# A fused attention and feed-forward kernel: the instruction order of all five engines written as one string, and 267 additions turned into accumulating transfers

## The chip, the cores and the metric

The kernel runs on one core of a Trainium2 chip. The core has five engines with a queue each: TensorE (PE; its weight loads are shown as PEld), VectorE (DVE), ScalarE (ACT), GpSimd (POOL) and SyncE (SP), which here only issues transfers. Each works through its queue in order and waits at the head for what the instruction needs. TensorE writes to PSUM, eight banks of 128 x 512 f32; the others work on SBUF, and all but GpSimd read PSUM as well. Transfers (DMAs) run on 16 transfer engines. The metric is the device time of one execution in microseconds, a median of several.

## The reference

An input x of 4 batches x 12416 rows x 128 channels goes through attention with 32 inducing points and then through a gated feed-forward layer of width 1536. All is float32.

```python
h = mab(I, x)                     # 32 rows per batch: softmax(I x^T / sqrt(C)) x
x = mab(x, h)                     # each row: softmax(x h^T / sqrt(C)) h
rms = sqrt(mean(x * x, -1) + 1e-6)
xn = x / rms * rms_g
g = xn @ w_gate                   # 128 -> 1536
silu = g * (1 / (1 + exp(-g)))
out = (silu * (xn @ w_val)) @ w_out   # 1536 -> 128
```

Since a row of x after the second attention is a weighting of the 32 rows of h, the kernel multiplies h with the gate and value weights once per batch (the stacks sg and sv), and a row then needs only its 32 weights, scaled by the root mean square.

## The kernel before, in words

Each batch b is cut into 7 sets of rows and these into 25 units: 24 of 512 or 480 rows and one of 256. A unit's weights lie in a tile a of 128 x 512: upper and lower halves of the 32 weights, twice, gathered by SyncE (`gather`, L560 on) from the halves that `seam` (L507 on) makes: turned scores, squares with the Gram matrix, a root on GpSimd, a scaling, and a split into an upper and a lower half.

A unit has 12 blocks j, one for each 128 columns of the 1536, 1200 blocks in all. `ffn` (L663 on) makes of each a slot: a gate matmul (L743, one pass, since a and sg are float32r), silu on ScalarE (L751), a value matmul (L754), and the product of silu and value on VectorE (L760). In 14 blocks that lie among the exponentials of attention, silu is put together from tanh (L747) and one more operation on VectorE (L748), so that ScalarE need not change its table.

The product u has then to be multiplied with 128 rows of w_out and summed over the 12 blocks in acc. A table of letters says in which of three ways:

- a dot, 381 blocks: plain. A float32 matmul, which TensorE runs as two instructions of two passes each (L676, acc<-u,wo).
- s, 619 blocks, "sums": u stays in the PSUM bank of the value. ScalarE takes an upper part from it (L725) and VectorE the remainder (L726), both float32r. GpSimd makes a third factor of the two in a third tile (L735). Three one-pass matmuls follow in `project3`: upper and lower into the bank u3 (L700, L702), the third into acc (L676).
- d, 200 blocks, "differences": u lies in SBUF; the upper part is made by ScalarE (L729), the remainder by GpSimd (L730), a scaling of the upper part by ScalarE (L734), and the third factor by GpSimd (L735).

w_out was split in the same way once (`split_wo`, `split_last`). When a unit's 12 products are done, ScalarE takes u3 (L705), VectorE adds acc (L685) and turns the result (L690), and SyncE stores it in four transfers (L717).

The factors u have 9 tiles. The sets of three tiles (upper, lower, third) number 4, and 2 more are lent from the stacks' buffers while the next batch's stacks are not being made. PSUM has 5 banks in turn for gates, values and attention, 2 for acc and 1 for u3.

While batch b goes through the blocks, the attention of batch b + 1 runs beside it in small steps (`attention`, L309 on): turns of the loaded channels, scores, maxima, exponentials, sums, stacks. A step often issues on several engines at once: `scores1` a matmul and VectorE's eviction, `stack` a matmul, a ScalarE copy and a VectorE subtraction, `turn_h` a matmul and two copies. The order is written out: `schedule` and `seams` say which steps there are, `places` in which slot each comes, `ordered` after which part of a slot how many plain and three-pass products are issued, `banks`, `workers` and `holders` which buffer each gets. `soon` and `wait` put a factor's making and a unit's finish one or two slots later.

The opening (`first`, L802 on) does batch 0's attention and rounds the weights, before the first block; the first 24 blocks go through two units side by side.

Of the kernel before, what the change touches and what calls it, by code (L numbers as in the profile page):

```python
# [23 lines left out]
def kernel(  # L24
# [75 lines left out]
    RING, RESERVE, HELD, SILU = 4, 7, 9, 3  # L100
    LENT = (RING, RING + 1)
# [41 lines left out]
    def load_channels(b, s, k):  # L143

        w = R * per[s]
        if not k:
            xT[b, s] = xtp.tile([P, w * m], F32, name=f"xT{s}")
        nc.sync.dma_start(out=xT[b, s][ts(k, m), :].rearrange("p (w c) -> p w c", c=m),
                          in_=xrows[ds(b * N + start[s], P * per[s]), ts(k, m)].rearrange("(i w) c -> i w c", i=m))
# [159 lines left out]
    def attention(b, load_next):  # L309
# [34 lines left out]
        def scores1(s):  # L344
            nc.vector.tensor_scalar(out=sc[b][:, cols1[s]], in0=scores(s, indT[:], R, per[s]), scalar1=1.0, scalar2=None,
                                    op0=ALU.mult, op1=ALU.max, accum_out=st["gmx"][:, s:s + 1])
# [31 lines left out]
        def sum_h(*sets):  # L378
# [12 lines left out]
            if b and sets[0]:  # L391
                nc.vector.tensor_tensor(out=hl[:, 0:C], in0=hl[:, 0:C], in1=ps[:, 0:C], op=ALU.add)
            elif b:
                nc.scalar.copy(out=hl[:, 0:C], in_=ps[:, 0:C])

        def fold_l():

            nc.vector.reduce_sum(out=st["hl"][:, C:C + 1], in_=st["ls"][:, 0:st["n"]], axis=AX.X)
            ps = bank()
            nc.tensor.matmul(ps[:, 0:1], fold[:].rearrange("p q m -> p (q m)"), st["hl"][:, C:C + 1], start=True, stop=True)  # L400
            rl = st["rl"] = small.tile([P, 1], F32, name="rl")
            nc.vector.reciprocal(out=rl[:], in_=ps[:, 0:1])
# [8 lines left out]
        def turn_h():  # L411

            ps = bank()
            nc.tensor.matmul(ps[:, 0:P], st["hn"], fold[:].rearrange("p q m -> p (q m)"), start=True, stop=True)
            hT = st["hT"] = once.tile([P, P], F32, name="hT")
            if b:
                nc.scalar.copy(out=hT[:], in_=ps[:, 0:P])
                hg = st["hg"] = once.tile([P, P], F32, name="hg")
                nc.scalar.activation(hg[:], ps[:, 0:P], AF.Copy, scale=gam)
            else:  # L420
                nc.vector.tensor_copy(out=hT[:], in_=ps[:, 0:P])
# [5 lines left out]
        def square_h():  # L427
# [4 lines left out]
            ps = bank()  # L432
            nc.tensor.matmul(ps[:, 0:m], st["hT"][:], st["hT"][:, 0:m], start=True, stop=True)
            for q in range(R):
                to, of_ = gram[b][ts(q, m), ts(q, m)], ps[ts(q, m), 0:m]
                nc.scalar.activation(to, of_, AF.Copy, bias=1e-6, scale=1.0 / C)

        def scores2(s):
            ps = scores(s, st["hT"][:, 0:m], quarters[s], per2[s])
            nc.vector.transpose(out=sc[b][rows2[s], cols2[s]], in_=ps)  # L440

        def row_max(s):
            mx = st["mx2"] = small.tile([P, 16], F32, name="mx2")[rows2[s], 0:per2[s]]
            nc.vector.reduce_max(out=mx, in_=weights(b, s), axis=AX.X)

        def sub_max(s):
            n, v, mx = per2[s], weights(b, s), st["mx2"]
# [16 lines left out]
        def stack(i):  # L464


            ps = bank()
            for c, w in enumerate(st.pop(("w", i))):
                nc.tensor.matmul(ps[ts(c, m), :], st["hg"][:, 0:m], w, start=True, stop=True)
            hi, lo = st["halves", i] = [worker([P, 512], F32R, n) for n in ("whi", "wlo")]  # L470
            rows = slice(0, NC * m)
            nc.scalar.copy(out=hi[rows, :], in_=ps[rows, :])
            nc.vector.tensor_tensor(out=lo[rows, :], in0=ps[rows, :], in1=hi[rows, :].bitcast(F32), op=ALU.subtract)
# [33 lines left out]
    def seam(b, s):  # L507
# [41 lines left out]
        def split():  # L549
# [4 lines left out]
            else:  # L554
                nc.vector.tensor_copy(out=hi[rows, 0:w], in_=aT[rows, 0:w])
            engine.tensor_tensor(out=lo[rows, 0:w], in0=aT[rows, 0:w], in1=hi[rows, 0:w].bitcast(F32), op=ALU.subtract)

        return [turn_a, square, times, scale, root, apply, turn_b, split]
# [11 lines left out]
    plain, kara, waiting = [], [], []  # L570

    def soon(k, step):

        waiting.append([k, step])

    def wait():

        for one in waiting:
            one[0] -= 1
        while any(not one[0] for one in waiting):  # L580
            one = next(one for one in waiting if not one[0])
            waiting.remove(one)
            one[1]()

    def give(group):

        for kind in group:
            (plain if kind == "p" else kara).pop(0)()

    def split_wo(step):  # L590

        if not step:
            kws["first"] = xnp.tile([P, half + NK, C], F32R, name=f"xn{full - 1}")
            rings = [xnp.tile([P, RING, 512], F32R, name=f"xn{full - 4 + n}") for n in range(3)]
            kws["sets"] = [[ring[:, n, :] for ring in rings] for n in range(RING)]
            idle.extend(range(RING))
# [10 lines left out]
        for g in range(2):  # L607
# [8 lines left out]
            if at == 4:  # L616
                nc.gpsimd.tensor_tensor(out=part(2, g)[0], in0=part(1, g)[1], in1=part(0, g)[1], op=ALU.subtract)
            if at == 6:
                scaled(0, g, 4096.0)

    idle, leaving = [], []

    def lend(b, k, idle, leaving):

        if k == (20 if not b else 2):
            idle += LENT
            return True
        if b + 1 < B and k == 184:
            leaving += [n for n in LENT if n not in idle]
            idle[:] = [n for n in idle if n not in LENT]  # L630
        assert k != 192 or not leaving

    def give_back(n, idle, leaving):

        leaving.remove(n) if n in leaving else idle.append(n)

    def lend_tiles():

        tiles = [stk.tile([P, F], F32R, name=name) for name in ("sg", "sv")]
        kws["sets"][RING:] = [[t[:, ts(n, 512)] for n in range(3)] for t in tiles]  # L640

    def split_last(step):

        n = NJ - NK
        if not step:
            kws["last"] = xtp.tile([P, 3 * n, C], F32R, name="xT0")
        one, (whi, wlo, ws) = wo[:, NK:NJ, :], (kws["last"][:, ts(kind, n), :] for kind in range(3))
        if step == 0:
            nc.scalar.activation(whi, one, AF.Copy, scale=1.0 - 2.0 ** -13)
            nc.gpsimd.tensor_tensor(out=wlo, in0=one, in1=whi.bitcast(F32), op=ALU.subtract)  # L650
        if step == 1:
            nc.scalar.activation(wlo, wlo.bitcast(F32), AF.Copy, scale=4096.0)
            nc.gpsimd.tensor_tensor(out=ws, in0=wlo.bitcast(F32), in1=whi.bitcast(F32), op=ALU.subtract)
        if step == 2:
            nc.scalar.activation(whi, whi.bitcast(F32), AF.Copy, scale=4096.0)

    def weight_of(kind, j):
        if j >= NK:
            return kws["last"][:, kind * (NJ - NK) + j - NK, :]
# [3 lines left out]
    def ffn(b, u):  # L663

        s, q = units[u]
        T = per2[s] * m
        a = moving.pop((b, u))
        sg, sv = stacks[b]
        acc = ps_acc.tile([P, 512], F32, name="acc")
        nk = sum((b, u, j) in kinds for j in range(NJ))  # L670
        st = {"left": NJ, "k": nk}
        if nk:
            st["o"] = None

        def project(lhsT, rhs, to):
            nc.tensor.matmul(to, lhsT, rhs, start=st["left"] == NJ, stop=st["left"] == 1)  # L676
            st["left"] -= 1
# [638 lines left out]
```

## Time and profile before

| | |
|---|---|
| median of 3 runs | 1538.12 us (1537.94 to 1538.22) |
| the profiled execution's own time | 1538.19 us |
| its span, first to last instruction | 1536.4 us |
| granted TensorE clock | 1.00 |
| instructions: VectorE, ScalarE, GpSimd | 2519, 2501, 1158 |
| transfers | 112.58 MB, 36.2% of 16 engines' span, all but a few issued by SyncE |
| the first gate of the feed-forward | 47.5 us after the start |
| the 27th gate | 84.3 us |
| start of batch 1, 2, 3 (its first gate) | 434, 805, 1180 us |

A line of a group reads: line of the kernel, engine, operation, what it writes <- what it reads, shapes, count | busy time, mean of one | idle time of the engine before them, and what ended it. A line of the waits reads: who <- whom: total us, times, the longest. A stage's limit is read from its own stretch, not from the total. A matmul's duration overlaps with the next one; the distance between starts is its price. "gv" are the five PSUM banks, "xn", "sg" and "sv" also name the sets of factors, which lie in buffers that had those names.

### The profile page before, as it was taken

Reading aid. Unit: us, or ns where it says so; the run is one execution under the profiler, and the core shown is the slowest. Engines: PE = TensorE matmul, PEld = TensorE weight load, DVE = VectorE, ACT = ScalarE, POOL = GpSimd, SP = SyncE. Lnnn points to the kernel's source line nnn. Section 1 sums busy time; section 2 is a strip of 40 time slices with the busy share of each in tenths; the row PEclk is TensorE's granted clock in tenths of the full one; section 3 lists DMA queues with packets and bytes.
Section 4 is the critical chain, followed back from the end, with each engine's and each line's share of the span. In section 5 each row is a group of like instructions: output and inputs, shape, how many; then the busy total and the mean of one; then the engine's idle time right before and its main releaser. Section 6 shows DMA issues by size and latency. Waiting matters only on the chain.

```text
span 1536.4 us, 26105 instructions
## 1 busy us (share of the span) xinstructions
PE 1518.3 (99%) x7141; PEld 1091.8 (71%) x7141; DVE 1442.3 (94%) x2519; ACT 1292.2 (84%) x2501; POOL 1418.5 (92%) x1158
## 2 busy tenths in 40 slices
PE   8999999999999999999999999999999999999998
PEld 6556667767776667776777667676677777777776
DVE  6999999999999998999999999899999999999997
ACT  5777889888888889887988888978798888888886
POOL 1379999999999999999999999899989999999997
PEclk9999999999999999999999999999999999999999
DMA  7345535435453242634444323353222222122221
GB/s 282 91 81 94 97 60 114 90 78 91 67 92 69 38 93 37 137 84 86 72 78 82 56 59 77 74 120 75 49 39 39 38 36 37 34 40 38 40 40 28
DMA packets 389331, 112.58 MB, mean 73 GB/s; under 512 B 365088, under 2 KB 369728, under 8 KB 386624
## 3 DMA queue, kind: packets, MB, share of 16 engines
q1 hardware_dynamic: 388592, 110.83, 36.2%
q8 instruction: 57, 0.93, 0.3%
q14 instruction: 90, 0.74, 0.2%
q10 hardware_dynamic: 592, 0.08, 0.0%
HBM read 53.95 MB, written 27.00 MB: 53 GB/s over the span
## 4 chain that ended last, share of the span: by engine, by line
PE 90%; DVE 3%; POOL 3%; ACT 2%; issue 1%; DMA 0%; DVEq 0%; POOLq 0%; ACTq 0%
PE acc L676 30%; PE gv L743 17%; PE gv L754 16%; PE u L700 10%; PE u L702 10%; PE gv L341 3%; PE gv L523 1%; PE gv L390 1%; POOL xn L735 1%; ACT silu L751 1%; PE gv L820 1%; DVE u L760 1%; POOL xn L730 0%; DVE gv L760 0%; DMA xn<-in_x_dram 0%
## 5 line engine op out<-in xcount | busy, mean ns | idle before, releaser
L735 POOL TENSOR_TENSOR xn<-xn,xn 128x512 fp32r<-128x512 f32 (+2 forms) x626 | 767.6, 1248 | 34.1 <-DVE xn L726 11.6
L751 ACT ACTIVATE silu<-gv 128x512 f32<-128x512 f32 (+2 forms) x1186 | 683.4, 588 | 98.4 <-PE gv L743 88.1
L754 PE MATMUL gv<-a,sv 128*128 128x512 f32 (+2 forms) x1188 | 551.2, 465 | 1.0 <-ACT silu L751 0.4
L743 PE MATMUL gv<-a,sg 128*128 128x512 f32 (+2 forms) x1188 | 472.2, 398 | 1.6 <-ACT silu L751 0.6
L760 DVE TENSOR_TENSOR gv<-silu,gv 128x512 f32<-128x512 f32 (+2 forms) x616 | 410.6, 673 | 23.4 <-PE gv L754 7.5
L760 DVE TENSOR_TENSOR u<-silu,gv 128x512 f32<-128x512 f32 (+2 forms) x570 | 369.4, 655 | 24.4 <-ACT silu L751 8.8
L676 PE MATMUL acc<-u,wo 128*128 128x512 f32 (+2 forms) x762 | 371.2, 577 | 0.0
L725 ACT ACTIVATE xn<-gv 128x512 fp32r<-128x512 f32 (+2 forms) x472 | 278.1, 589 | 62.3 <-DVE gv L760 47.2
L726 DVE SCALAR_TENSOR_TENSOR xn<-xn,gv 128x512 fp32r<-128x512 f32 (+2 forms) x472 | 312.5, 662 | 13.1 <-ACT xn L725 7.4
L743 PEld LDWEIGHTS gv<-a,sg 128*128 128x128 f32 x1188 | 224.1, 189 | 137.4 <-issue 26.7
L754 PEld LDWEIGHTS gv<-a,sv 128*128 128x128 f32 x1188 | 224.3, 189 | 116.5 <-ACT silu L751 34.4
L700 PE MATMUL u<-xn,xn 128*128 128x512 f32 (+2 forms) x599 | 233.7, 390 | 0.0
L676 PE MATMUL acc<-xn,more 128*128 128x512 f32 (+2 forms) x599 | 225.7, 377 | 1.4 <-POOL xn L735 1.2
L730 POOL TENSOR_TENSOR xn<-u,xn 128x512 fp32r<-128x512 f32 (+2 forms) x154 | 191.0, 1240 | 5.1 <-ACT xn L729 4.7
L676 PEld LDWEIGHTS acc<-u,wo 128*128 128x128 f32 x762 | 142.9, 190 | 32.2 <-issue 15.4
L700 PEld LDWEIGHTS u<-xn,xn 128*128 128x128 f32 x599 | 113.3, 189 | 25.6 <-ACT o L705 8.0
L676 PEld LDWEIGHTS acc<-xn,more 128*128 128x128 f32 x599 | 113.1, 189 | 24.4 <-POOL xn L735 10.2
L735 POOL TENSOR_TENSOR sg<-sg 128x512 fp32r<-128x512 f32 (+2 forms) x97 | 123.4, 1272 | 3.6 <-DVE sg L726 1.0
L735 POOL TENSOR_TENSOR sv<-sv 128x512 fp32r<-128x512 f32 (+1 forms) x96 | 122.1, 1272 | 1.6 <-DVE xT L324 0.2
L702 PE MATMUL u<-xn,more 128*128 128x512 f32 (+2 forms) x304 | 113.0, 372 | 0.0
L702 PE MATMUL u<-xn,xn 128*128 128x512 f32 (+2 forms) x295 | 109.8, 372 | 0.0
L729 ACT ACTIVATE xn<-u 128x512 fp32r<-128x512 f32 (+2 forms) x154 | 95.3, 619 | 14.2 <-DVE u L760 9.2
(229 smaller groups left out, 1894.7 us busy)
## 6 DMA issues: line engine op xcount, KB each, us to landing
out_dram<-o SPq DMA_DIRECT2D x320, 64.0 KB, 2.0
xT<-in_x_dram SPq DMA_DIRECT2D x60, 256.0 KB, 3.9
xn<-in_x_dram SPq DMA_DIRECT2D x60, 256.0 KB, 5.0
a<-hi SPq DMA_DIRECT2D x156, 64.0 KB, 2.0
a<-lo SPq DMA_DIRECT2D x156, 64.0 KB, 2.0
xn<-in_x_dram SPq DMA_DIRECT2D x5, 1024.0 KB, 9.7
xn<-w SPq DMA_DIRECT2D x18, 256.0 KB, 3.0
out_dram<-o SPq DMA_DIRECT2D x64, 60.0 KB, 2.0
```

What stands on the lines that cost most here:

```text
L676: nc.tensor.matmul(to, lhsT, rhs, start=st["left"] == NJ, stop=st["left"] == 1)
L700: nc.tensor.matmul(ups[:, 0:T], weight_of(0, j), halves_in_turn(hi), start=st["k"] == nk, stop=False)
L702: nc.tensor.matmul(ups[:, 0:T], weight_of(1, j), halves_in_turn(lo), start=False, stop=not st["k"])
L725: nc.scalar.activation(hi, v, AF.Copy, scale=(1.0 - 2.0 ** -13) * 2.0 ** -12)
L726: nc.vector.scalar_tensor_tensor(out=lo, in0=hi.bitcast(F32), scalar=-4096.0, in1=v, op0=ALU.mult, op1=ALU.add)
L729: nc.scalar.activation(d, v, AF.Copy, scale=1.0 - 2.0 ** -13)
L730: nc.gpsimd.tensor_tensor(out=lo, in0=v, in1=d.bitcast(F32), op=ALU.subtract)
L735: nc.gpsimd.tensor_tensor(out=d, in0=hi.bitcast(F32), in1=lo.bitcast(F32), op=ALU.subtract)
L743: nc.tensor.matmul(g[:, 0:T], sg[:, ts(j, P)], halves_in_turn(a[:, 0:T]), start=True, stop=True)
L751: nc.scalar.activation(sl[:, 0:T], g[:, 0:T], AF.Silu)
L754: nc.tensor.matmul(v[:, 0:T], sv[:, ts(j, P)], halves_in_turn(a[:, 0:T]), start=True, stop=True)
L760: nc.vector.tensor_tensor(out=t[:, 0:T], in0=sl[:, 0:T], in1=v[:, 0:T], op=ALU.mult)
```

## The change

1. **Order.** Slots, `soon`, `wait`, `schedule`'s slots and the table of products are gone, but for the first 26 blocks, which keep their order. After these a string `program` of 10,695 letters is run from left to right, and each letter issues one step on one engine: g gate, s silu, y tanh, x the operation after tanh, v value, m product, h upper part, l lower part on VectorE, n lower part on GpSimd, e scaling of the upper part, q two of the three passes, d the third factor by GpSimd, D the third factor by a transfer, r and R the third pass behind d and D, p a plain product, E, F, T, O a unit's four finishing steps, a gather, and a dot for the next of attention's steps by the list `taken`.
2. **Steps of one engine.** Attention's steps that used several engines are split: `scores1` and `evict1`, `scores2` and `turn2`, `sum_h` and `take_h`, `fold_l` in three, `turn_h` and two copies, `square_h` and `copy_gram`, `stack`, `stack_high` and `stack_lower`, and the split of a seam into `split` and `lower`.
3. **Kinds.** `sorts` has a letter for each block: 366 plain, 586 sums (412 S, 174 s), 248 differences (155 D, 93 d). A small letter means that the third factor is made by a transfer: 267 blocks. 28 blocks use tanh.
4. **Third factor in place.** The signs of the upper parts are turned, so that the third factor is the sum of upper and lower part and can be put over the lower part, after the first two passes have read it: by GpSimd (567 blocks), or by a transfer that GpSimd issues and that adds the upper part's 128 x 512 f32 to the lower part in SBUF. A three-pass block thus has two tiles instead of three.
5. **Buffers.** 9 tiles for u and 10 more, 19 in one pool for plain factors, upper and lower parts. Nothing is lent from the stacks. The last split of w_out lies beside them and is made in the opening.

VectorE's lower part is taken from PSUM alone, as before.

```diff
-        RING, RESERVE, HELD, SILU = 4, 7, 9, 3
-    LENT = (RING, RING + 1)
+    RING, HELD, SILU = 4, 9, 3
...
-            rings = [xnp.tile([P, RING, 512], F32R, name=f"xn{full - 4 + n}") for n in range(3)]
-            kws["sets"] = [[ring[:, n, :] for ring in rings] for n in range(RING)]
+            rings = [xnp.tile([P, RING * 512], F32R, name=f"xn{full - 4 + n}") for n in range(3)]
+            kws["room"] = [ring[:, ts(n, 512)] for ring in rings for n in range(RING)][:3 * RING - 2]
...
-                nc.gpsimd.tensor_tensor(out=d, in0=hi.bitcast(F32), in1=lo.bitcast(F32), op=ALU.subtract)
-                kara.append(lambda: project3(j, where))
...
+    def high():
+        n = lists["h"].pop(0)
+        one, kind, t = unit_of(*blocks[n][:2]), kinds[n], factor_of[n]
+        T = one["T"]
+        hi = t["hi"] = room()[:, 0:T]
+        t["lo"] = room()[:, 0:T]
+        if kind in "Dd":
+            nc.scalar.activation(hi, t["u"], AF.Copy, scale=1.0 - 2.0 ** -13)
+            lists["n"].append(n)
+        else:
+            nc.scalar.activation(hi, t["u"], AF.Copy, scale=-(1.0 - 2.0 ** -13) * 2.0 ** -12)
+            lists["l"].append(n)
...
+    def low():
+        nc.vector.scalar_tensor_tensor(out=t["lo"], in0=t["hi"].bitcast(F32), scalar=4096.0, in1=t["u"],
+                                       op0=ALU.mult, op1=ALU.add)
...
+    def low_of_u():
+        nc.gpsimd.tensor_tensor(out=t["lo"], in0=t["u"], in1=t["hi"].bitcast(F32), op=ALU.subtract)
...
+    def project_two():
+        nc.tensor.matmul(ups, weight_of(0, j), halves_in_turn(t["hi"]), start=not one["q"], stop=False)
+        nc.tensor.matmul(ups, weight_of(1, j), halves_in_turn(t["lo"]), start=False, stop=last)
+        one["q"] += 1
+        lists["D" if kinds[n].islower() else "d"].append(n)
...
+    def add_in_place():
+        n = lists["d"].pop(0)
+        t = factor_of[n]
+        nc.gpsimd.tensor_tensor(out=t["lo"], in0=t["hi"].bitcast(F32), in1=t["lo"].bitcast(F32), op=ALU.add)
+        lists["r"].append(n)
+
+    def add_by_transfer():
+        n = lists["D"].pop(0)
+        t = factor_of[n]
+        nc.gpsimd.dma_start(out=t["lo"].bitcast(F32), in_=t["hi"].bitcast(F32), accum_op=ALU.add)
+        lists["R"].append(n)
+
+    def project_third(name):
+        n = lists[name].pop(0)
+        project(n, weight_of(2, blocks[n][2]), halves_in_turn(factor_of[n]["lo"]), False)
...
+    program = """
+        .p.gg.EE.vps..s.g.av.g.vpmm.gpFy..py..h.xpyx....mvlghpmyn.TvqhxpO.D.egpmsFvgxqp.dsvmgvl.phmsrg.Rvsg.mvq.sgvDpm
...
+    for name in "".join(program.split()):
+        if name == ".":
+            step, args = micros[int(next(taken))]
+            step(*args)
+        else:
+            do[name]()
```

## The prediction

> **What bounds the kernel now.** I read the page's totals and its 40 slices first, then the chain that ended last, then the busy time by stretch, the waits, the groups, and TensorE's timeline for prices.
>
> ```profile
> PE 1518.3 (99%) x7141; PEld 1091.8 (71%) x7141; DVE 1442.3 (94%) x2519; ACT 1292.2 (84%) x2501; POOL 1418.5 (92%) x1158
> ...
> PE 90%; DVE 3%; POOL 3%; ACT 2%; issue 1%; DMA 0%; DVEq 0%; POOLq 0%; ACTq 0%
> ```
> ```profile
> 1300.00:1400.00 100.00, 99.97 (x404) 74.24 (x403) 97.00 (x161) 87.59 (x167) 98.52 (x78) 1.00 0.20 36
> ```
> Columns of the second: stretch, length, then PE, PEld, VectorE, ScalarE, GpSimd busy, clock, transfer share, GB/s. Three engines stand at 97% or more there, only ScalarE has room, and the clock is full. TensorE's 99% flatters it, since its ends are modelled; its own work has to be counted from starts:
>
> ```profile
> 1323.46 0.38 PE L700 MATMUL u<-sv,xn 128*128 128x512 f32 x1
> 1323.68 0.38 PE L702 MATMUL u<-sv,more 128*128 128x512 f32 x1
> 1323.90 0.38 PE L676 MATMUL acc<-sv,more 128*128 128x512 f32 x1
> 1324.11 1.02 PE L676 MATMUL acc<-u,wo 128*128 128x512 f32 x2
> 1324.57 0.78 PE L754 MATMUL gv<-a,sv 128*128 128x512 f32 x1
> 1325.19 0.38 PE L743 MATMUL gv<-a,sg 128*128 128x512 f32 x1
> ```
> A one-pass matmul starts 0.215 us after the last; the plain product (0.38 to 0.215 apart around it) takes 1325.19 - 1324.11 - 0.215 = 0.865. With 2400 gates and values and 3 x 819 products in passes, at a mean width of 496.6 of 512: 4857 x 0.209 = 1014; 381 plain x 0.84 = 320; attention's matmuls by their lines' shares of the chain (2.9, 1.5, 1.1, 0.7%) and small ones some 112. So TensorE works about 1446 of 1536 us and waits 90. By counts in the same way some 27 of these lie in the first 100 and last 37 us, which leaves **62 us of short waits** spread over the middle. Who ends them:
>
> ```profile
> ACT silu L751 <- PE gv L743: 88.1, 148, 3.0
> ACT xn L725 <- DVE gv L760: 47.2, 93, 1.6
> PEld gv L754 <- ACT silu L751: 35.8, 117, 1.1
> ...
> PEld gv L743 <- ACT silu L751: 25.1, 80, 0.9
> PEld gv L743 <- DVE xn L726: 17.8, 64, 0.8
> ...
> PEld gv L743 <- DVE u L760: 15.5, 42, 0.8
> ...
> PEld acc L676 <- POOL xn L735: 11.0, 31, 0.9
> ```
> Of the weight loads' waits that name an engine, some 155 us, VectorE ends 62 (17.8, 15.5, 12.0, 7.6 and small ones), ScalarE 80, GpSimd 13. A weight load stands early in the queue, so its wait is not all TensorE's: I share the 62 us alike, 25 to VectorE, 32 to ScalarE, 5 to GpSimd. GpSimd's queue is nearly full, but few wait for it.
>
> **The change, part by part.** The prices of the other engines:
>
> ```profile
> L735 POOL TENSOR_TENSOR xn<-xn,xn 128x512 fp32r<-128x512 f32 (+2 forms) x626 | 767.6, 1248 | 34.1 <-DVE xn L726 11.6
> ...
> L726 DVE SCALAR_TENSOR_TENSOR xn<-xn,gv 128x512 fp32r<-128x512 f32 (+2 forms) x472 | 312.5, 662 | 13.1 <-ACT xn L725 7.4
> ...
> L730 POOL TENSOR_TENSOR xn<-u,xn 128x512 fp32r<-128x512 f32 (+2 forms) x154 | 191.0, 1240 | 5.1 <-ACT xn L729 4.7
> ```
> *Kinds of product.* The letters count 381 plain, 619 sums, 200 differences before; 366, 586 and 248 after. TensorE: 15 plain become three passes, 15 x (0.84 - 0.63) = **-3.2 us**, all on the path. VectorE: 33 lower halves fewer, -33 x 0.66 = -21.8; 28 tanh blocks for 14, each with one more operation of 0.67: +9.4; together -12.4. ScalarE: 15 upper halves and 48 scalings more at 0.6: +38 us, inside the 16% that it idles; this cover goes only where exponentials stand (14 changes of table in the string and 2 in the opening, the 16 loads of 1.28 us of before).
>
> *Third factors.* 819 additions on GpSimd become 567, and 267 transfers that GpSimd issues. -252 x 1.24 = -312.5; 48 subtractions more, +59.5; so its busy time goes from 1418.5 to 1165.5 + 267 X, with X the time that one issue holds GpSimd. Before has none. Bounds: SyncE issues a 256 KB transfer of 128 rows (the weights' fetch) in 0.43 us; above, the 1.24 of the addition replaced. GpSimd takes 1.25 for what VectorE does in 0.66, so I double SyncE's 0.43 to 0.53 and estimate X at 0.95: 1419, as before. At 0.43 it is 1280, at 1.24 1497. The Trainium skill, *DMA: Bandwidth & Descriptors*, "SWDGE vs HWDGE vs iDMA" and "Specifications", says that code on GpSimd's cores writes these descriptors, first byte after about 1 us against 0.6. An estimate from that page, X = 1.0, would make it 1433; no row here shows it. The sum now goes over the lower part, so every third factor, 834 of them, waits for TensorE's first two passes, which it did not before; behind it in GpSimd's queue stand further additions, subtractions and attention's scalings, and behind those TensorE's third passes.
>
> *Landing.* The fetch lands in 2.6 to 4.0 us, median 3.0, issue included; with the longer issue 3.5. How far the third pass stands behind its transfer I take from TensorE's letters between the two, at 0.215 for a pass and 0.865 for a plain product: median 4.1 us, a tenth under 3.2. 48 of 267 are under 3.5, by 23 us in sum. Attention's matmuls and waits lie between too and are not in it, so half: **+10 us** where TensorE, in order, stands. Ends: 0 and, at a landing of 4.5, the whole 126 us. Bytes: 267 x 0.25 MB = 68 MB beside 112.6; the first slice moves 282 GB/s at a share of 0.7, some 400 at full, so +11% of share to 36%, +22% if adding moves them twice: room on the mean, less in stretches at 0.45.
>
> *The loop in place.* The same count for the 567 additions gives a median of 1.29 us of TensorE's work from addition to third pass, and the addition lasts 1.25: no slack. Before, GpSimd's share of the 62 us was 5; I double it: **+5 us**. Ends: 0 and 90, the sum of what the pairs fall short of 1.3 us.
>
> *Order.* Loads hardly move, so the time is in the 62 us of waits. Steps that came as a fixed group in a slot now stand singly on each engine. VectorE's 12.4 us less work should take half of its 25: -12. ScalarE waits 88 us for gates while idle 16%, which is order and not work; singly placed steps take, I judge, a little over half of its 32: -18. Together **-30 us**; ends 0 and -57 (all but GpSimd's 5). Against it: 9 + 10 buffers serve where 9 and 18 did, and a room freed by a third pass is given out again within the same block in 272 of 828 cases, so ScalarE's next upper half waits close behind TensorE. I count that inside the range.
>
> *SyncE.* It issues the same loads, gathers, placements and stores, in the string's order. Its longest wait by far is this:
>
> ```profile
> SPq L717 <- DVE o L690: 435.7, 66, 13.3
> ```
> Stores hold its queue until an output is turned, and gathers and loads stand behind. Gathers come 10 blocks (a block lasts (1532 - 84) / 1174 = 1.23 us, so 12.3) ahead of their unit in nearly all cases, about as before, and take 2.0 us to landing, so 10 us cover them and I cost the new order at 0; one gather held for the longest wait above, 13.3 us, would come 3 us late.
>
> *Opening and end.* The first 26 blocks keep their order, banks and products; the tail still ends in store and drain: 0.
>
> **Sum.** The profiled execution took 1538.2 us (span 1536.4 and 1.8 around), the median being 1538.1: 1538.2 - 3.2 - 30 + 10 + 5 = **1520 us**.
>
> **The rivals.** *GpSimd binds (slower).* Its queue is full in the middle and its work grows where X exceeds 0.95. If every us of it is then a us of the span, X = 1.1 gives 1538 + 40 = 1578, X = 1.24 1617; if the queue were held to the landing at 3.0 us, 1538 + 267 x 2.05 = 2085, the change then not doing what it says. For it: 98.5% busy above. Against: only 13 us of weight-load waits name it. The Trainium skill, *Perfetto Trace Analysis*, "Identifying the Most-Contended Engine", asks to optimise the engine of highest occupancy first; by that rule this rival, not the waits' order, sets the time. The waits in the trace do not bear it out.
> *Third passes late (slower).* At a landing of 4.5 us half of 126 stands for 10: 1520 + 53 = 1573; in stretches without loads less, with the tight rooms passing each stop on to ScalarE more. For it: loads of x land in 3.9 and 5.0 us, and the string keeps no slack. Decisive from a landing of about 4.0 us, where half the shortfall (55 us) takes the 28 us that the other terms gain. Against: 4.1 us is the median distance.
> *Waits mostly go (faster).* -50 instead of -30, and no late third pass: 1538 - 3 - 50 = 1485. Against: TensorE's own work remains at 1443 us, its ends at 27.
> *Nothing moves.* The order gains what the third passes cost: 1536.
>
> **How the numbers follow.** Forecast, 1503 to 1534: 0.35; waits mostly go: 0.14; nothing moves: 0.06; third passes late: 0.23; GpSimd binds: 0.22. Faster is 0.35 + 0.14 = 0.49, slower 0.45. Under 0.2% (3 us) a measurement of this kernel can hardly tell from none. The range goes from 1488, short of the best case, to 1595, past late landings and X = 1.1; the forecast's own is 1503 to 1534.
>
> **What would show it.** Right: VectorE's busy time near 1430, lower halves' group x586, GpSimd near 1420 or less with 267 issues near 0.95, waits of weight loads on ScalarE and VectorE below 155 us in sum, third passes seldom ended by a transfer. Wrong: issues above 1.1 us; TensorE's matmuls waiting on a DMA for more than 20 us; ScalarE's upper halves waiting on TensorE's third passes; additions and issues on GpSimd waiting on TensorE's two passes.

## The result, and the profile after

The changed kernel takes **1585.25 us** (median; 1584.31 to 1591.39) against 1538.17 us for the kernel before on the same chip: ratio **1.031** with a 95% interval of 1.0287 to 1.034. It is 47 us slower where 18 us faster was forecast; the time lies inside the range. The profiled execution took 1584.31 us, with a span of 1582.5.

The page's totals, the queue of the new transfers and the chain that ended last:

```profile
PE 1531.6 (97%) x7156; PEld 1088.1 (69%) x7156; DVE 1437.6 (91%) x2500; ACT 1323.5 (84%) x2564; POOL 1407.9 (89%) x1221
...
q0 software_dynamic: 38448, 67.98, 25.0%
...
PE 61%; POOL 14%; DMA 8%; DVE 6%; issue 5%; ACT 4%; SPq 1%; POOLq 0%; DVEq 0%; ACTq 0%
```

VectorE and GpSimd are less busy than before, GpSimd by 10.6 us, and ScalarE, 31.3 us busier, still idles for 16%. But the chain has gone from 90% TensorE to 61%, and GpSimd's share from 3% to 14%. Two of GpSimd's groups, additions and issues (busy us, mean ns of one | idle before):

```profile
L789 POOL TENSOR_TENSOR u<-xn,u 128x512 fp32r<-128x512 f32 (+2 forms) x287 | 435.3, 1563 | 26.5 <-PE u L770 18.4
...
L795 POOL DMA_DIRECT2D xn<-xn x139 | 160.0, 1179 | 13.1 <-issue 2.2
```

The addition shows 1.56 us where it had 1.25. The waits (us in total, times, the longest):

```profile
PEld acc L781 <- POOL u L789: 62.6, 128, 2.6
PEld acc L781 <- POOL xn L789: 52.3, 126, 1.3
...
PEld acc L781 <- DMA xn<-xn: 16.9, 22, 2.7
PEld acc L781 <- DMA u<-xn: 7.6, 16, 1.2
```

L781 under "acc" is the third pass. Before, its waits on GpSimd's additions were 11.0 us in the largest group. Weight loads wait on silu less than before, for 11.4 us ahead of gates and 9.1 ahead of values, where 25.1 and 35.8 stood. A count from TensorE's starts (the distance between two starts, less the median for the same matmul between the same neighbours) puts its waits ahead of third passes at 5.5 us before and 64 after, and all the others together, the opening's included, at 118 and 106. The two changes add up to 46 us, and the span grew by 46.1. (The 38 us that an expectation below names come from a rougher count, which went by each matmul's width and left some 10 us unplaced.)

### The profile page after: what moved, and what is told of

Read it like the earlier page. It is cut to its first block, busy times and chain, and to the rows that moved or that the text cites. A ratio compares the mean times of both kernels' runs of the same rounds, so it can differ in the third digit from the quotient of the medians.

```text
span 1582.5 us, 26222 instructions
## 1 busy us (share of the span) xinstructions
PE 1531.6 (97%) x7156; PEld 1088.1 (69%) x7156; DVE 1437.6 (91%) x2500; ACT 1323.5 (84%) x2564; POOL 1407.9 (89%) x1221
## 4 chain that ended last, share of the span: by engine, by line
PE 61%; POOL 14%; DMA 8%; DVE 6%; issue 5%; ACT 4%; SPq 1%; POOLq 0%; DVEq 0%; ACTq 0%
PE acc L781 21%; PE gv L682 11%; PE gv L710 10%; PE u L769 7%; PE u L770 7%; POOL u L789 4%; DMA xn<-xn 4%; POOL xn L789 3%; DMA u<-xn 2%; POOL xn L750 2%; PE gv L340 2%; ACT silu L692 2%; DVE gv L724 1%; POOL xn L795 1%; POOL rs L560 1%
## 5 line engine op out<-in xcount | busy, mean ns | idle before, releaser
L710 PE MATMUL gv<-a,sv 128*128 128x512 f32 (+2 forms) x1188 | 478.6, 404 | 0.7 <-DVE xn L743 0.4
L789 POOL TENSOR_TENSOR u<-xn,u 128x512 fp32r<-128x512 f32 (+2 forms) x287 | 435.3, 1563 | 26.5 <-PE u L770 18.4
L724 DVE TENSOR_TENSOR gv<-silu,gv 128x512 f32<-128x512 f32 (+1 forms) x579 | 383.0, 675 | 36.9 <-PE gv L710 28.4
L781 PE MATMUL acc<-u,wo 128*128 128x512 f32 (+2 forms) x732 | 359.6, 576 | 0.0
L789 POOL TENSOR_TENSOR xn<-xn,xn 128x512 fp32r<-128x512 f32 (+2 forms) x231 | 340.0, 1511 | 20.5 <-PE u L770 19.7
L769 PE MATMUL u<-xn,xn 128*128 128x512 f32 (+2 forms) x788 | 302.5, 384 | 4.4 <-ACT o L822 2.6
L743 DVE SCALAR_TENSOR_TENSOR u<-xn,gv 128x512 fp32r<-128x512 f32 (+2 forms) x307 | 203.6, 665 | 7.8 <-ACT xn L737 6.2
L756 ACT ACTIVATE xn<-xn 128x512 fp32r<-128x512 f32 (+2 forms) x246 | 152.8, 622 | 47.6 <-POOL xn L750 24.9
L743 DVE SCALAR_TENSOR_TENSOR xn<-xn,gv 128x512 fp32r<-128x512 f32 (+2 forms) x278 | 183.7, 665 | 8.0 <-ACT xn L737 7.4
L750 POOL TENSOR_TENSOR u<-u,xn 128x512 fp32r<-128x512 f32 (+2 forms) x108 | 171.9, 1616 | 10.1 <-ACT xn L734 8.6
L769 PEld LDWEIGHTS u<-xn,xn 128*128 128x128 f32 x788 | 149.2, 189 | 33.8 <-ACT xn L756 9.0
L795 POOL DMA_DIRECT2D xn<-xn x139 | 160.0, 1179 | 13.1 <-issue 2.2
L781 PE MATMUL acc<-xn,more 128*128 128x512 f32 (+2 forms) x340 | 159.9, 474 | 8.1 <-POOL xn L789 3.8
L781 PE MATMUL acc<-u,more 128*128 128x512 f32 (+2 forms) x345 | 155.0, 455 | 8.7 <-POOL u L789 6.5
```

The costliest lines, as they stand in the source:

```text
L710: nc.tensor.matmul(v[:, 0:T], stacks[b][1][:, ts(j, P)], halves_in_turn(one["a"][:, 0:T]), start=True, stop=True)
L724: nc.vector.tensor_tensor(out=to, in0=sl[:, 0:T], in1=v[:, 0:T], op=ALU.mult)
L743: nc.vector.scalar_tensor_tensor(out=t["lo"], in0=t["hi"].bitcast(F32), scalar=4096.0, in1=t["u"], op0=ALU.mult, op1=ALU.add)
L750: nc.gpsimd.tensor_tensor(out=t["lo"], in0=t["u"], in1=t["hi"].bitcast(F32), op=ALU.subtract)
L769: nc.tensor.matmul(ups, weight_of(0, j), halves_in_turn(t["hi"]), start=not one["q"], stop=False)
L781: nc.tensor.matmul(to.rearrange("p (n h) -> p h n", h=2) if step2 else to, lhsT, rhs, start=one["left"] == NJ, stop=one["left"] == 1)
```

## The experiments

All times stand against the kernel before at 1537.6 to 1538.3 us beside them. The first runs asked what the transfers cost and where it is waited for. Their result led to the theory called Q in all texts that name it: a transfer's issue holds GpSimd's queue, and what stands behind comes late. Its rivals change with what is asked.

### What the transfers cost, and what they save

`no_transfer`, the transfer left out:

```diff
-        nc.gpsimd.dma_start(out=t["lo"].bitcast(F32), in_=t["hi"].bitcast(F32), accum_op=ALU.add)
```

> The changed kernel (1585 us) without its 267 accumulating transfers: nothing is issued in their place, and those third passes read the lower part without the sum (267 of 834 sums are left out). Takes away the issue on GpSimd, the traffic and the wait for the landing at once. Theory 'landing' (third passes wait for transfers that land after 4.1 us) and theory 'late additions' (after an issue GpSimd's additions end later, and third passes wait for these) both expect most of the 47 us back: 1535 to 1550. Theory 'order' (the string itself is worse than the slots, and the third passes are only where it shows) expects at least 1570.

`add_for_transfer`, an addition in its place:

```diff
-        nc.gpsimd.dma_start(out=t["lo"].bitcast(F32), in_=t["hi"].bitcast(F32), accum_op=ALU.add)
+        nc.gpsimd.tensor_tensor(out=t["lo"], in0=t["hi"].bitcast(F32), in1=t["lo"].bitcast(F32), op=ALU.add)
```

> The changed kernel with an addition on GpSimd in place of each transfer, at the same place of the string. From the trace an issue takes some 0.86 us of GpSimd from end to end, an addition 1.24, so GpSimd has 267 x 0.38 = 101 us more. 'Late additions' and GpSimd's queue as the bound expect 1630 to 1690. 'Landing' expects the waits for transfers to go and at most half of the 101 to show: 1560 to 1620. 'Order' expects 1585 plus what GpSimd adds, some 1640.

Measured: 1505.68 us without (ratio 0.979, 0.9773 to 0.9802), 1622.41 us with additions (1.0544, 1.0528 to 1.0559). So the rest of the change, with these 267 sums left out, is 32.5 us faster than before, and the 267 transfers cost **79.6 us** on top of it; additions would cost 116.7. Neither time was expected: 1505.7 is below what all three theories gave, and 1622.4 lies between 'landing' (up to 1620) and the other two (from 1630). Without transfers the page has:

```profile
PE 1490.2 (99%) x7156; PEld 1098.9 (73%) x7156; DVE 1419.2 (94%) x2500; ACT 1313.0 (87%) x2564; POOL 1176.7 (78%) x954
...
PE 95%; DVE 2%; ACT 1%; issue 1%; POOL 1%; DMA 0%; SPq 0%; DVEq 0%; ACTq 0%; POOLq 0%
```

GpSimd lost 231 us, 0.87 for each transfer, and TensorE's waits ahead of third passes are 5.0 us by the count from starts.

### Which third passes wait

Third passes read a constant in place of their factor: those behind transfers (`R_reads_weights`), those behind additions (`r_reads_weights`), all (`both_read_weights`).

```diff
+        lo = factor_of[n]["lo"]
+        if name == "R":
+            lo = kws["more"][:, 0:4, :].rearrange("p k c -> p (k c)")[:, 0:lo.shape[-1]]
-        project(n, weight_of(2, blocks[n][2]), halves_in_turn(factor_of[n]["lo"]), False)
+        project(n, weight_of(2, blocks[n][2]), halves_in_turn(lo), False)
```

> The changed kernel, but the 267 third passes behind a transfer read 512 columns of a constant in SBUF, so they don't wait for the landing; the transfer is still issued, moves its bytes and holds its rooms. Those 267 sums are left out of the output. 'Landing' expects the most of this one: 1545 to 1560. 'Late additions' expects 1570 to 1580 (of the waits of third passes' weight loads some 25 us of 140 end with a transfer). 'Order': 1575 to 1585.

> The changed kernel, but the 567 third passes behind GpSimd's additions read the constant, so they don't wait for the addition; additions and transfers are all still made. Those 567 sums are left out of the output. 'Late additions' expects 1545 to 1560, most of the 38 us that TensorE stands ahead of third passes; 'landing' expects 1575 to 1585; 'order' 1575 to 1585.

> All 834 third passes read a constant in place of their factor, so the projection is wrong; every transfer, addition and issue stays, but TensorE waits for none of them. Taken alone, the two halves gained 15.2 us (transfers) and 8.4 us (additions). Theory Q, with the delay in GpSimd's queue reaching the other kinds of work too (the halves that are subtracted, the spaces that come free): the two together give 1545 to 1565 us. If the third passes' own waits were all of it: 1500 to 1515 us.

Measured: 1570.03, 1576.85 and 1551.86 us. Waiting for transfers alone is worth 15.2 us, for additions 8.4, for both 33.4. 'Landing' had put the first run at 1545 to 1560 and 'late additions' the second, and both missed, because where one wait is taken away, the other grows: weight loads of third passes wait for transfers 54.9 us in `r_reads_weights`, where 24.5 stood, and for additions 127.0 us in `R_reads_weights`, where 114.9 stood. And 46.2 of the 79.6 us stay when no third pass waits for anything. They come another way round: GpSimd's subtractions are late, ScalarE's scaling (L756) waits for them, and TensorE's first pass (L769) for the scaling. In `both_read_weights`:

```profile
ACT xn L756 <- POOL xn L750: 37.0, 51, 2.1
ACT xn L756 <- POOL u L750: 31.2, 43, 2.8
PEld u L769 <- ACT xn L756: 25.9, 45, 2.3
```

Without transfers the first two are 3.9 and 4.7 us.

### The issue or the data

`narrow_transfer` adds 32 columns, `tiny_transfer` 32 columns of one partition, `sp_copy` lets SyncE move the same bytes.

```diff
-        nc.gpsimd.dma_start(out=t["lo"].bitcast(F32), in_=t["hi"].bitcast(F32), accum_op=ALU.add)
+        nc.gpsimd.dma_start(out=t["lo"].bitcast(F32)[:, 0:32], in_=t["hi"].bitcast(F32)[:, 0:32], accum_op=ALU.add)
...
+        nc.gpsimd.dma_start(out=t["lo"].bitcast(F32)[0:1, 0:32], in_=t["hi"].bitcast(F32)[0:1, 0:32], accum_op=ALU.add)
...
+        nc.sync.dma_start(out=t["lo"].bitcast(F32), in_=t["hi"].bitcast(F32))
```

> Each of the 267 transfers adds only 32 of its 512 (or fewer) columns, so the third factors are wrong in the other columns; the issue on GpSimd, the order and the waits stay, the data falls to a sixteenth. Theory Q (GpSimd's queue: each issue holds it for about 0.86 us and delays what stands behind it): the time stays near the changed kernel's, 1565 to 1588 us, less by at most the landing's own share. Rival T (the transfers' data: their 25% of the DMA engines, their landing of 4.1 us): 1510 to 1540 us, near the 1505.7 us of the run without transfers.

> Each of the 267 transfers adds 32 columns of one partition only, in the same place of GpSimd's order and behind the same wait for TensorE's two passes; the rest of those third factors stays unsummed. Theory Q (the time that an issue holds GpSimd's queue): the time follows the length of the issue as its row shows it: with an issue of 0.2 us or less 1505 to 1520 us, with an unchanged 0.86 us the 1572.3 us of the narrow transfers. Rival W (an instruction that stands in GpSimd's queue and waits there for the two passes, however short): 1560 to 1575 us with a short issue too.

> Each of the 267 transfers is issued by SyncE as a plain copy of the upper part over the lower part, so those third factors hold the upper part alone; the bytes written stay, GpSimd issues nothing. Theory Q: GpSimd falls to about 1180 us busy, the landings' wait stays: 1512 to 1535 us. Rival T: the data still moves and lands late: 1570 to 1590 us. SyncE's own fetches now queue behind waits for TensorE's two passes; if that binds, the time would be above both and TensorE would be seen waiting on fetched tiles.

Measured: 1572.27, 1550.34 and 1515.48 us. A sixteenth of the data takes 13.0 us of the 79.6 away; the same number of bytes issued by SyncE takes 69.8. SyncE's copies also land sooner, after 2.3 us; but the tiny transfers land as soon (2.2 to 2.3 us), move next to nothing, and are 34.9 us slower. It is the issue on GpSimd that costs. The tiny transfers' issues were not short, so the case that would have told theory Q from rival W did not come about, and 1550.3 us lies below W's 1560 to 1575 and Q's 1572.3 for an unchanged issue; L795 of `tiny_transfer`:

```profile
L795 POOL DMA_DIRECT2D xn<-xn x139 | 138.0, 1015 | 14.9 <-PE u L770 3.5 <-ACT silu L692 3.1 <-PE gv L682 1.9
```

From idle such an issue takes 0.77 us (median of 68) where the whole transfer's takes 0.87: the length hardly follows the data. For the two passes an issue seldom waits at the queue's head, 5.5 us in all in the changed kernel and 7.0 in `tiny_transfer`, so rival W has little to stand on. Yet GpSimd is busy for 1381.0 us in place of the narrow transfers' 1407.5, and the time is 21.9 us lower for these 26.5: at this load 0.83 us of the span for each us of GpSimd, an upper value, since the landing went from some 2.65 to 2.25 us too.

### Fewer transfers, and a GpSimd with room

`every_second` leaves out every second transfer; `half_adds` halves the 567 additions; `half_adds_narrow` and `half_adds_no_transfer` do that with narrow transfers and with none.

```diff
-        nc.gpsimd.dma_start(out=t["lo"].bitcast(F32), in_=t["hi"].bitcast(F32), accum_op=ALU.add)
+        kws["skip"] = not kws.get("skip", False)
+        if not kws["skip"]:
+            nc.gpsimd.dma_start(out=t["lo"].bitcast(F32), in_=t["hi"].bitcast(F32), accum_op=ALU.add)
...
+        half_ = slice(0, t["lo"].shape[-1] // 2)
-        nc.gpsimd.tensor_tensor(out=t["lo"], in0=t["hi"].bitcast(F32), in1=t["lo"].bitcast(F32), op=ALU.add)
+        nc.gpsimd.tensor_tensor(out=t["lo"][:, half_], in0=t["hi"][:, half_].bitcast(F32), in1=t["lo"][:, half_].bitcast(F32), op=ALU.add)
```

> Every second transfer is left out (134 of 267; those third factors stay unsummed). If each transfer has a price of its own, however full GpSimd is: 1505.7 + 79.6/2 = 1545 us. Theory Q with a queue near its limit (GpSimd at 1290 us instead of 1408): the price is paid by the last ones, 1515 to 1532 us.

> The 567 additions on GpSimd take the first half of the columns only (the other half of those third factors stays unsummed); all 267 transfers and 248 subtractions stay. GpSimd loses some 567 x 0.55 = 310 us. Theory Q: with GpSimd near 1100 us the transfers cost little beyond their landing, 1510 to 1530 us. Rival I (an issue costs what it costs wherever GpSimd stands, by its landing and by lengthening its neighbours): 1560 to 1585 us.

> The additions take half the columns and the transfers add 32 of 512 columns (the rest of those third factors stays unsummed): GpSimd relieved as in half_adds (1117 us busy, 1549.8 us), the issues as they were, the landing 2.7 us after the issue's start instead of 4.0. Theory L (with GpSimd relieved, what is left of the transfers' price is their landing): 1512 to 1527 us. Rival I (the issues themselves and what they do to their neighbours): 1538 to 1550 us.

> The additions take half the columns and all transfers are left out (third factors unsummed): what the kernel takes when GpSimd has neither, the base that half_adds is to be held against. Both theories: 1500 to 1506 us, TensorE's own work; if it were well under 1500 us the transfers' price at a relieved GpSimd would be larger than the 44 us that the 1505.7 us run gives.

`every_second` took 1535.0 us (ten runs, 1532.4 to 1538.1), between what the two theories gave: with 133 transfers the price is 29.3 us, and the other 134 add 50.3, so the price grows with GpSimd's load, though less steeply than theory Q had it. `half_adds` fell between both theories, and its two companions settle it. Median us, GpSimd's busy time in brackets:

| | additions whole | additions halved |
|---|---|---|
| no transfer | 1505.7 (1176.7) | 1503.2 (880.3) |
| 32 columns, landing 2.7 / 2.4 us | 1572.3 (1407.5) | 1524.0 (1116.5) |
| whole transfer, landing 4.1 / 4.0 us | 1585.3 (1407.9) | 1549.8 (1116.6) |

With room on GpSimd, issues and a short landing cost 20.8 us and the longer landing 25.8. At the full queue, issues and a short landing cost 66.6 and the longer landing only 13.0: GpSimd is late by then with other things too, so part of the landing lies beside. **Taken in this order, the full queue is 45.8 of the 79.6 us and the longer landing 13.0**, and 20.8 remain with issues that have room. Taken the other way, with the additions halved under whole transfers first, the queue is 33.0 and the landing 25.8: the two overlap. In `half_adds` third passes wait more on the transfers themselves (32.8 us) than on additions (24.8, where 114.9 stood):

```profile
PEld acc L781 <- DMA xn<-xn: 17.8, 18, 3.3
...
PEld acc L781 <- DMA u<-xn: 15.0, 21, 2.8
PEld acc L781 <- POOL u L790: 14.3, 33, 2.1
...
PEld acc L781 <- POOL xn L790: 10.5, 25, 0.8
```

### The place of the third pass

`late_R` moves each letter R in the string `program` up to 6 places back, by at most half the way to where its space is taken again or its unit is finished. The string's first line:

```diff
-        .p.gg.EE.vps..s.g.av.g.vpmm.gpFy..py..h.xpyx....mvlghpmyn.TvqhxpO.D.egpmsFvgxqp.dsvmgvl.phmsrg.Rvsg.mvq.sgvDpm
+        .p.gg.EE.vps..s.g.av.g.vpmm.gpFy..py..h.xpyx....mvlghpmyn.TvqhxpO.D.egpmsFvgxqp.dsvmgvl.phmsrg.vsg.mvRq.sgvDpm
...
```

`four_passes` does without transfers; TensorE multiplies upper and lower part with the third weights:

```diff
-        nc.gpsimd.dma_start(out=t["lo"].bitcast(F32), in_=t["hi"].bitcast(F32), accum_op=ALU.add)
...
+        if name == "R":
+            project(n, weight_of(2, blocks[n][2]), halves_in_turn(factor_of[n]["hi"]), False, whole=False)
+            unit_of(*blocks[n][:2])["begun"] = True
         project(n, weight_of(2, blocks[n][2]), halves_in_turn(factor_of[n]["lo"]), False)
```

> The whole computation; each third pass behind a transfer stands up to 6 letters (3.4 on the average, about 0.5 us) later in the string, as far as half the way to where its space is taken again. If the landing's wait is what costs, 267 passes with 0.5 us more room take some of the 44 us of third passes' waits away: 1565 to 1580 us. If GpSimd's queue sets the pace, the time moves by less than 5 us: 1580 to 1590 us, and the waits for the spaces grow.

> The whole computation, without transfers: for the 267 blocks TensorE multiplies the third weights by the upper and by the lower part, two passes in place of one over their sum. 267 x 0.216 = 57.6 us more on TensorE than the run without transfers: 1505.7 + 57.6 = 1563 us (1558 to 1570), 22 us below the changed kernel if the transfers' price of 79.6 us is GpSimd's and the landing's, as theory Q has it. Rival: the third passes' place in the order is what costs, and the longer stay of TensorE there adds to it: 1580 to 1600 us.

Measured: 1584.72 and 1557.22 us. In `late_R` the third passes' waits went down on the transfers and hardly on the additions, and nothing was gained:

```profile
PEld acc L781 <- POOL u L789: 59.3, 128, 2.6
PEld acc L781 <- POOL xn L789: 49.4, 114, 1.7
...
PEld acc L781 <- DMA xn<-xn: 9.4, 9, 3.4
PEld acc L781 <- DMA u<-xn: 6.5, 9, 1.5
```

So at the full queue the queue sets the pace. `four_passes` pays 51.5 us for 267 passes (0.193 each, 6 less than expected) and does the whole computation 28.0 us faster than the transfers do; against the kernel before it is still slower (1.0127, 1.0112 to 1.0142). Since a transfer costs 0.30 us of the span on the average, a pass of TensorE is the cheaper way, though TensorE is the busiest engine.

### Differences made plain: a miss

`plain_D60` makes 60 of the D blocks plain products, which takes 120 operations off GpSimd and leaves all 267 transfers; `no_transfer_D60` is the same without transfers. In the string h, n, e, d and r of these blocks go, and z, the plain product, stands where q stood, or earlier where the space is taken again before; the list of who gets which buffer is made anew for it.

```diff
-                             "k": sum(kind != "P" for kind, one in zip(kinds, blocks) if one[:2] == (b, u)), "ups": None,
+                             "k": sum(kind not in "PZ" for kind, one in zip(kinds, blocks) if one[:2] == (b, u)), "ups": None,
...
-        lists["p" if kind == "P" else "h"].append(n)
+        lists["p" if kind == "P" else "z" if kind == "Z" else "h"].append(n)
...
-        PsDsPdPPsDPSPPDDSDPSSDSPDdPSDSSPSdPsDPdsddPDPPDPPSsdsSPSSPPSdPPSsDDDsDPSSPPPDSPDSSSSSSPSSSdSDPsPsdSsPPSSDPPSDP
+        PsZsPdPPsDPSPPZDSDPSSZSPDdPSZSSPSdPsDPdsddPDPPZPPSsdsSPSSPPSdPPSsDZDsDPSSPPPZSPDSSSSSSPSSSdSDPsPsdSsPPSSZPPSDP
...
-        .p.gg.EE.vps..s.g.av.g.vpmm.gpFy..py..h.xpyx....mvlghpmyn.TvqhxpO.D.egpmsFvgxqp.dsvmgvl.phmsrg.Rvsg.mvq.sgvDpm
+        .p.gg.EE.vps..s.g.av.g.vpmm.gpFy..py..h.xpyx....mvlgpmy.TvqhxpO.D.gpmsFvgxzp.svmgvl.phmsg.Rvsg.mvq.sgvDpmnmhgp
...
```

> 60 of the 155 differences with an addition by GpSimd become plain products, evenly spread: GpSimd loses 60 subtractions and 60 additions (about 60 x 2 x 1.28 to 1.56 = 154 to 187 us), ScalarE 120 activations, TensorE gains 60 x 0.21 = 13 us; all 267 transfers stay as they are, and the whole computation. Theory Q: with GpSimd near 1240 us busy most of the 79.6 us that the transfers cost goes: 1520 to 1545 us, against the kernel before a gain or no change. Rival T: the transfers cost what they did, and the longer products are added: 1575 to 1600 us.

> The 60 differences made plain products once more, now with all 267 transfers left out. It prices the edit of plain_D60 (1592.1 us) by itself. If its price is TensorE's longer products alone: 1505.7 + 13 = 1516 to 1523 us, and then the 70 us of plain_D60 above it are the transfers', at a GpSimd busy for only 79% of the span. If the edit has a price of its own (the space for u is held until the plain product has read it; VectorE waited 17.1 us for that): 1530 to 1565 us, and plain_D60 says little on the transfers.

Measured: 1592.12 and 1526.52 us. The edit alone costs 20.8 us, between its two expectations and some 8 more than TensorE's longer products (VectorE also waits for the spaces of u: 17.1 us in `plain_D60`, 12.1 without transfers). With that taken off, the transfers still cost 65.6 us, at a GpSimd that is busy for 1263.7 of 1590 us. I had expected that most of the price goes with a fifth of GpSimd's time free. It doesn't, and so a busy share averaged over the span isn't the measure. Third passes still wait on both kinds there:

```profile
PEld acc L781 <- POOL u L789: 40.8, 80, 2.6
PEld acc L781 <- POOL xn L789: 34.7, 83, 1.3
PEld acc L781 <- DMA u<-xn: 16.4, 23, 4.1
PEld acc L781 <- DMA xn<-xn: 11.8, 14, 3.6
```

Why halved additions relieve so much more (46.6 us left at 1116.6) than 120 operations fewer (65.6 at 1263.7) is not settled. The time from an addition's end to its third pass differs as the prices do: in `half_adds` it is 1.13 us (median), and 26 of 567 start within 0.2 us; in `plain_D60` it is 0.32, and 170 of 507 do. That this room sets the price, and that it comes from every addition being shorter, is only argued; no run tells it apart.

## Why the prediction was wrong

**The step that failed is "Third factors".** Its sizes were right: GpSimd was put at 1419 us busy and has 1407.9; X was put at 0.95 and is 0.87 by the busy times (1407.9 - 1176.7, over 267). But it gave the issues no price, because GpSimd stays as busy "as before", and because "GpSimd's queue is nearly full, but few wait for it". That held for the kernel before only. There, a third pass starts 1.12 us (median) after its addition has ended, and 59 of 819 within 0.2; without transfers in the new order it is 0.52; in the changed kernel 0.21, and 252 of 567 within 0.2. (Paired in order of issue, which is the order in which both come.) Equal load, a fifth of the room: a delay in GpSimd's queue now reaches TensorE. (The step from 0.52 to 0.21 is of the size of the lag that an issue leaves behind it, 0.3 us, shown in the last section.) Measured, 66.6 of the 79.6 us come with narrow transfers already.

**"The loop in place"**, +5 with ends 0 and 90, had seen this: "no slack" between addition and third pass. Alone it was small, as forecast: 5.0 us of waits ahead of third passes when no transfers are issued, 5.5 before. The mistake was to price the two steps apart. The loop's missing slack gives the issues the larger part of their price; 20.8 us remain where GpSimd has room.

**"Landing"**, estimated 3.5 us and +10, was mis-sized: it is 4.0 to 4.2 us. What it has beyond the narrow transfers' 2.6 to 2.7 us is worth 13.0 us at the full queue and 25.8 with room on GpSimd, within the ends 0 and 126. The text's decisive point, 4.0 us, was met, though not alone.

**"Order"**, -30, came out as far as the runs can show it. Without transfers the kernel is 32.5 us faster than before; with TensorE's -3.2 and the loop's 5, -30 gives 28.2. But GpSimd has some 240 us less to do there than in the kernel that was forecast, so this is the gain of the order and of a relieved GpSimd together; no run shows the order alone. ScalarE's silu ends far less of the weight loads' waits, as it had to be. The 155 us of such waits that the forecast shared out are short of the sum, since they leave the view's smaller rows aside: all rows give 213 (ScalarE 102, VectorE 91, GpSimd 20), in much the same proportions, so the shares stand. In the changed kernel ScalarE and VectorE end 125 of them and GpSimd 120. VectorE's work fell by 4.7 us in the changed kernel, not by 12.4, and ScalarE's rose by 31.3, not 38; neither decides. TensorE's -3.2 is too small for a count from starts to tell.

**SyncE at 0** is not contradicted: its loads landed later beside the transfers (xT 3.9 to 4.8 us, a 2.0 to 2.5), but with the data cut to a sixteenth (4.1 and 2.0) only 13.0 us came back, and these hold the third passes' own landing.

**The rivals.** "GpSimd binds" had the mechanism, at 0.22, with a wrong condition: it asked for an X above 0.95, and it came true at 0.87 with less busy time than before. Its price, a us of the span for each us, is near the 0.83 measured. That the time lies inside the range is luck in part: the upper end stood for landings later than these and an X of 1.1. The rule of the Trainium skill, *Perfetto Trace Analysis*, "Identifying the Most-Contended Engine", stood beside that rival: improve the engine of highest occupancy first. Beside TensorE, which the rule judges otherwise, it names GpSimd from 1300 to 1400 us in both kernels, at 98.5% before and at 96.0% after. In the one few waited for it, in the other it decided, so in this stretch the rule points at the right engine for the kernel after, and occupancy doesn't tell the two kernels apart. Over the whole span it names VectorE in both (94% and 91%, against GpSimd's 92% and 89%). "Third passes late" is the smaller part of what happened.

```profile
1300.00:1400.00 100.00, 97.38 (x396) 71.75 (x395) 91.01 (x149) 88.37 (x170) 95.99 (x83) 1.00 0.50 87
```

That is the stretch after, in the columns of the one before. Of the signs set out for "wrong", TensorE's waits on a transfer came only with those of weight loads, 34.6 us in all, 10.1 for matmuls; alone they would have blamed the landing. Issues above 1.1 us came in one row alone, 1.18 us for 139 of them (1.08 for the other 128), and that row counts an overlap twice (last section). The waits of GpSimd's additions for the two passes (45.3 us) say the contrary of what I took them for: without transfers, when GpSimd has room, they are 132.5. The plain sign, third passes that wait for additions, wasn't among them.

Put together: 1538.2 - 32.5 + 66.6 + 13.0 = 1585.3. The terms are differences between these very runs, so the sum shows where the time went and confirms nothing beyond them.

## What to carry to other kernels

A queue's busy share tells what it can still take in, not what a delay in it costs; for that, measure the time between each result and its reader, before and in the new order. A DMA that an engine has to issue is work of that engine: price it like an instruction on its queue, at its place in every loop that runs through that queue, and not by its bytes alone. And two steps that share a queue aren't to be priced apart: a loop without slack is cheap alone, and dear as soon as something is put into it.

## What the runs showed of the hardware

An issue on GpSimd lasts 0.87 us from idle for 256 KB and 0.77 for 128 bytes (medians). The next instruction starts some 0.26 us before the issue's end and is shown 0.3 us longer, and so is each one behind it until GpSimd idles. In `every_second` (start, us, instruction):

```profile
1306.41 0.91 POOL L797 DMA_DIRECT2D xn<-xn  x1 [2.85 <-PE gv L710]
1307.06 1.57 POOL L789 TENSOR_TENSOR u<-xn,u 128x512 fp32r<-128x512 f32 x1
1308.28 1.57 POOL L750 TENSOR_TENSOR u<-u,xn 128x512 fp32r<-128x512 f32 x1
1309.51 1.57 POOL L750 TENSOR_TENSOR xn<-u,xn 128x512 fp32r<-128x512 f32 x1
```

Starts are 1.23 us apart, as without transfers (1.24), so the 1.57 is not a slower addition (without transfers it is 1.28): the results come 0.3 us later. The lag adds up: in the changed kernel 512-column additions and subtractions take 1.28 us (median) with no issue since GpSimd last idled, 1.55 to 1.56 behind one, 1.85 behind two. And it is real: of third passes behind additions of 1.75 us and more, over half start within 0.07 us of the end shown, and none before it. The durations of single instructions count the overlap twice: GpSimd's add up to 1803 us where the page's total has 1407.9.

From the issue's start to the landing it took 4.0 to 4.2 us for the accumulating 256 KB in the changed kernel (3.6 to 3.7 in `every_second`), 2.6 to 2.7 for 16 KB and 2.2 to 2.3 for 128 bytes. In the page of the changed kernel:

```profile
xn<-xn POOLq DMA_DIRECT2D x118, 256.0 KB, 4.2
u<-xn POOLq DMA_DIRECT2D x102, 256.0 KB, 4.0
```

The Trainium skill, *DMA: Bandwidth & Descriptors*, "Anatomy of one DMA — SWDGE (gpsimd) path", has 2.0 us and the bytes at 436 GB/s, by which an estimate for these is 2.6 us; the accumulating transfers here took 1.4 to 1.6 us more, and the measurement decides. A plain copy of the same tiles that SyncE issued landed in 2.3 us.
